# v's split parts stored by ScalarE in thirds, and k and q asked for later, in an attention and mixture-of-depths kernel

## The chip, the cores and the metric

The kernel runs on one core of a Trainium2 chip. Its metric is the device time of one execution in microseconds (us). Engines are named as the profile names them: PE (TensorE's matmuls), PEld (its weight loads), DVE (VectorE), ACT (ScalarE), POOL (GpSimd) and SP (SyncE, which here only issues transfers). Each takes its instructions in the order in which the program wrote them, and waits on semaphores where an operand is not ready. A transfer (DMA) is issued by SP, ACT or POOL and carried out by 16 DMA engines.

## The reference

An attention block whose keys and values are first condensed to 32 memory slots per head, and then a feed-forward block that works on 128 of the 576 rows of each batch. `q`, `k`, `v` are (8, 8, 576, 64), `phi` is (8, 8, 576, 32), all float32; the second block has width 512 and a hidden width of 1024.

```python
a = exp(phi - phi.max(axis=2)); a = a / (a.sum(axis=2) + 1e-9)     # softmax over the 576 rows
k_m, v_m = einsum('bhsm,bhsd->bhmd', a, k), einsum('bhsm,bhsd->bhmd', a, v)
scores = q @ k_m.transpose(0, 1, 3, 2) / 8
attn = softmax(scores)                                             # over the 32 slots
x = (attn @ v_m) with heads side by side                           # (8, 576, 512)
s = x @ w_gate
for b in range(8):
    top = the 128 rows of b with the largest s[b]
    out[b] = x[b]
    out[b, top] += sigmoid(s[b, top]) * (relu(x[b, top] @ w1) @ w2)
```

## The kernel before

The 64 pairs of batch and head are taken four heads at a time: 16 *groups* (b, g), numbered 0 to 15, two per batch.

**Softmax and keys** (`softmax`, L187, and `keys`, L306). A group's weights `a` are computed by DVE and ACT in turn on tiles of 128x576, with many correction steps. `load_phi` (L98) fetches phi when the group starts. `load_k` (L102, called at L228) fetches the group's k, 576 KB, into the tile `kb`. At the end `keys` transposes `a` on PE (L314), splits it on DVE in a coarse part and a rest (`big`, `low`, L320 and L322), has POOL store both parts to the DRAM tensor `aparts` (8 transfers, L325), and multiplies with `kb` on PE (L331) into `kbd`, the condensed keys.

**Splitting v** (`split_v`, L284). For each group a piece of v is loaded by SP into the tile `vb` (L291). DVE makes the coarse part `vhi` (L294) and the rest, in place in `vb` (L296). POOL stores both to the DRAM tensor `vparts` (L298), each written twice: a stored piece is twice what was read. The first nine groups go in whole pieces (1152 columns) with two buffers; the other seven go in halves (576 columns) with one buffer. Nothing reads `vb` afterwards but the two stores, so a buffer is free when both have landed.

**Sums of values** (`all_sums`, L355). v's condensed form needs more precision than one pass over the parts gives, so the parts of `a` and v are read back as rows spread over 32 partitions and multiplied by PE in a fixed order of rows (L382, tiles `acc`). There are four *stages*, each for two batches (four groups), and 32 pieces of 18 rows in a stage. `load_rows` (L341) has SP issue five transfers per piece: one of `v_rows` from vparts (L344) and four of `a_rows` from aparts (L351), into one of three sets of buffers. A stage's first rows are asked for when all its four groups have been done for five turns (L367), and its sums begin two turns after that at the earliest.

**Attention** (`attention`, L676). For a batch: `centre` (DVE, PE, ACT), `scores` (PE multiplies q with `kbd`, L490; ACT and DVE make exp minus one, L476 to L479), `attend` (PE L535 and L548, DVE L552, POOL or DVE L555, and POOL's stores of `out` and `xs`), `rank` (DVE and ACT find each row's rank) and `gather` (POOL fetches the chosen rows). q of the next batch is fetched by `load_q` (L106) into two buffers `qb`: at L683, in the two calls that follow the scores. A batch's attention may start when its sums are done, when fewer than two others are running, and 12 turns after the last start (8 when softmax is over).

**Feed-forward** (`ffn`, L636). PE's products with `w1_sb` (L654) and `w2_sb` (L664), and a scattered store into `out`.

**The order of the work** is written out by a loop of *turns* at the end of the kernel function. All the parts above are Python generators; each `yield` ends a *call*. A turn makes one call of softmax (two groups alternate in the first part, one runs alone later; a group takes ten calls), then perhaps one of `split_v`, then 7, 10 or 12 of `all_sums` (`steps`, L730; eight matmuls each), then one for each running attention, then two of the feed-forward. That order is the order of instructions on every engine and in every queue; times come out of it and of the waits. SP's queue therefore holds, turn by turn, the loads of phi and k, of v, of rows and of q. Counted by the yields, the loop has 226 turns. The first part ends at turn 83, when the odd groups below 8 are done: the tiles of the first part are given up, v goes on in halves, and attention may begin. Softmax is done in turn 160.

`split_v` has two yields per piece: a call that loads, and a call that splits and stores. It is called at every fourth turn in the first part and at every second later (L763). So a split comes four turns after its load, then two, and a group takes eight turns in both.

Of the kernel before, what the change touches and what calls it, by code (L numbers as in the profile page):

```python
# [39 lines left out]
def kernel(  # L40
# [15 lines left out]
    nc = tc.nc  # L56
# [45 lines left out]
    def load_k(i, ch):  # L102
        ks[i] = exs[ch].tile([PT, NC, D // NG], F32, name="kb")
        nc.sync.dma_start(out=ks[i], in_=k[groups[i]])

    def load_q(b, j):  # L106
        qs[b, j] = step.tile([P, NPR, S // 2], F32, name="qb")
        nc.sync.dma_start(out=qs[b, j], in_=qT[b, :, :, j * (S // 2):(j + 1) * (S // 2)])
# [78 lines left out]
    def softmax(i, ch):  # L187

        ex = exs[ch]

        def t(name, dtype=F32):

            return ex.tile([P, NC * P if name in WIDE else S], dtype, name=name)[:, :S]

        r = phis.pop(i)
        less_mx = ex.tile([P, 1], F32, name="mx")
        nc.vector.tensor_scalar(out=t("den"), in0=r, scalar1=-1.0, scalar2=None, op0=ALU.mult,
                                op1=ALU.min, accum_out=less_mx)
        nc.scalar.activation(r, r, AF.Identity, bias=less_mx)
        q = t("q", I16)  # L200
        act(q, r, LOG2E)
        yield
        for ln2 in (LN2_HI, LN2_LO):
            stt(out=r, in0=q, scalar=-ln2, in1=r, op0=ALU.mult, op1=ALU.add)

        rh, rl = t("rh", I16), t("rl")
        act(rh, r, 2.0 ** 11)
        num, den = t("num"), t("den")
        act(num, r, SQ[0], SQ[1], AF.Square)
        act(den, r, EXP_Q[2] * UP, EXP_Q[1] * UP)  # L210
        ends = t("lo"), t("big")
        act(ends[0], rh, -0.2734375 * UP * GRID, UP)
        act(ends[1], rh, UP * GRID / 4, EXP_P[1] * UP)
        yield
        stt(out=num, in0=num, scalar=SQ[2], in1=r, op0=ALU.add, op1=ALU.mult)
        act(num, num, 1.0, EXP_P[2] * UP)
        stt(out=rl, in0=rh, scalar=-GRID, in1=r, op0=ALU.mult, op1=ALU.add)

        def near(val, f, end):


            low = t("low")
            stt(out=low, in0=val, scalar=-f * UP, in1=r, op0=ALU.add, op1=ALU.mult)
            stt(out=low, in0=rl, scalar=f * UP, in1=low, op0=ALU.mult, op1=ALU.add)
            tt(out=val, in0=end, in1=low, op=ALU.add)

        yield
        load_k(i, ch)  # L228
        near(den, -0.2734375, ends[0])
        dh = t("dh", I16)  # L230
        act(dh, den, FINE)
        near(num, 0.25, ends[1])
        vh = t("vh", I16)
        act(vh, num, GRID)
        y0 = t("y0", I16)
        act(y0, r, 1.0, 14 * LN2, AF.Exp)
        inv = t("rl2")
        act(inv, r, INV[0], INV[1], AF.Exp)
        act(inv, inv, 1.0, INV[2] - 9 * LN2, AF.Exp)
        yield  # L240


        lo, big, low = t("lo"), t("big"), t("low")
        tt(out=low, in0=num, in1=rl, op=ALU.mult)
        stt(out=lo, in0=num, scalar=GRID, in1=vh, op0=ALU.mult, op1=ALU.subtract)
        tt(out=lo, in0=lo, in1=rh, op=ALU.mult)
        tt(out=big, in0=vh, in1=rh, op=ALU.mult)
        tt(out=low, in0=low, in1=lo, op=ALU.add)
        stt(out=num, in0=big, scalar=UP, in1=low, op0=ALU.add, op1=ALU.add)
        yield  # L250

        dl, p = t("lo"), t("big")
        stt(out=dl, in0=den, scalar=FINE, in1=dh, op0=ALU.mult, op1=ALU.subtract)
        tt(out=p, in0=y0, in1=dh, op=ALU.mult)
        tt(out=num, in0=num, in1=p, op=ALU.subtract)
        tt(out=dl, in0=y0, in1=dl, op=ALU.mult)
        tt(out=num, in0=num, in1=dl, op=ALU.subtract)
        two_q = t("den", I32)
        yield
        act(two_q, q, UP, 127 * UP, AF.Relu)  # L260
        tt(out=num, in0=num, in1=inv, op=ALU.mult)
        tt(out=num, in0=num, in1=y0, op=ALU.add)
        sm = ex.tile([P, 4], F32, name="sm")
        e = num
        stt(out=e, in0=num, scalar=FINE, in1=two_q.bitcast(F32),
            op0=ALU.mult, op1=ALU.mult, accum_out=sm[:, 0:1])

        nc.vector.tensor_scalar_add(sm[:, 0:1], sm[:, 0:1], 1e-9)
        nc.vector.reciprocal(sm[:, 1:2], sm[:, 0:1])  # L269
        nc.vector.tensor_single_scalar(sm[:, 2:3].bitcast(I32), sm[:, 0:1].bitcast(I32), -4096,  # L270
                                       op=ALU.bitwise_and)
        nc.vector.tensor_sub(sm[:, 3:4], sm[:, 2:3], sm[:, 0:1])
        nc.vector.tensor_scalar_mul(sm[:, 2:3], sm[:, 2:3], -1.0)
        a0 = t("vh", F16)
        nc.scalar.activation(a0, e, AF.Copy, scale=sm[:, 1:2])  # L275
        yield
        for part in (2, 3):
            stt(out=e, in0=a0, scalar=sm[:, part:part + 1], in1=e, op0=ALU.mult, op1=ALU.add)
        stt(out=e, in0=e, scalar=sm[:, 1:2], in1=a0, op0=ALU.mult, op1=ALU.add)  # L279
        soft[i] = e  # L280
        yield
        yield from keys(i, ch)

    def split_v(some, pool, cuts):  # L284

        n = 4 * S * Dh // P
        for b, g in some:
            for x0 in range(0, n, n // cuts):
                x = slice(x0, x0 + n // cuts)
                vb = pool.tile([P, n // cuts], F32, name="vb")  # L290
                nc.sync.dma_start(out=vb, in_=v[b, g, :, x])  # L291
                yield
                hi = pool.tile([P, n // cuts], F32, name="vhi")
                nc.vector.tensor_single_scalar(hi.bitcast(I32), vb.bitcast(I32), -4096,  # L294
                                               op=ALU.bitwise_and)
                nc.vector.tensor_sub(vb, vb, hi)  # L296
                for vp, src in enumerate((vb, hi)):
                    nc.gpsimd.dma_start(  # L298
                        out=vparts[b, g, :, vp].rearrange("w r s d -> w (r s d)")
                                               .rearrange("w (p x) -> p w x", p=P)[:, :, x],  # L300
                        in_=src.unsqueeze(1).to_broadcast([P, 2, n // cuts]))
                yield
# [52 lines left out]
    def all_sums():  # L355
# [7 lines left out]
        def load_some(end):  # L363
            while len(loaded) < min(end, len(pieces)):
                st, ch = pieces[len(loaded)]

                if not all(turn >= made.get(i, turn) + 5  # L367
                           for i in range(st * SET * NG, (st + 1) * SET * NG)):
                    break
                load_rows(len(loaded), st, ch)  # L370
                loaded.append(turn)
# [155 lines left out]
    def attend(b, general):  # L527
        eT, tg = eTs[b % 2], tgs[b % 3]
        row, rest = mean[b]
        for c0 in range(0, NT, 2):  # L530
# [5 lines left out]
                                     rhs=heads_of, start=True, stop=True)  # L536
            if working:
                yield
            rd = step.tile([P, 2, H], F32, name="rd")[:, :cols]
            nc.vector.tensor_scalar(out=rd.rearrange("p c (g h) -> p c g h", g=2), in0=den,  # L540
                                    scalar1=float(M), scalar2=1e-9, op0=ALU.add, op1=ALU.add)
# [134 lines left out]
    def attention(b, general=False):  # L676
        yield from centre(b)
        yield
        yield from (scores_less_max if general else scores)(b)
        for j in range(2):  # L680
            yield
            if not general and b + 1 < B:
                load_q(b + 1, j)  # L683
        yield from attend(b, general)
        yield
        yield from rank(b)
        for t in range(nt):
            yield from gather(b, t)
            chosen.append((b, t))
# [63 lines left out]
    while True:  # L753
# [6 lines left out]
        if working and next(working[0], working) is working:  # L760
            finish(working[1])
            working.clear()
        if working and turn % (2 if attend_all else 4) == 1:  # L763
            next(working[1], None)
        for _ in range(steps()):
            next(sums, None)
        if attend_all is None and set(order[1]) <= set(made):

            finish(working[1])
            first.close()  # L770
            work, step, one = (
                ctx.enter_context(tc.tile_pool(name=name, bufs=2 - (name == "one"),
                                               reuse_waits="tile"))
                for name in ("step", "work", "one"))
            vio = ctx.enter_context(tc.tile_pool(name="vio2", bufs=1, reuse_waits="tile"))
            working[1] = split_v(groups[two + 1:], vio, 2)
            for j in range(2):
                load_q(0, j)
            eTs = [one.tile([P, 2, NT * P], F32, name=f"eT{i}") for i in range(2)]
            for t in eTs:  # L780
                nc.gpsimd.memset(t[:, :, S:], 0.0)
            attend_all = attentions()
# [54 lines left out]
```

## Time and profile before

| | us |
|---|---|
| median of 9 runs (lowest to highest) | 914.66 (901.18 to 927.58) |
| the profiled execution | 910.61 |
| its span, first to last instruction | 908.8 |
| PE busy in it | 600.8 |
| DVE busy | 611.8 |
| ACT busy | 295.0 |
| POOL busy | 235.2 |
| the four stages of sums on PE, begin to end | 142 to 292, 296 to 435, 486 to 621, 667 to 782 |
| start of softmax of groups 8, 10, 12, 14 (DVE, L197) | 246, 333, 444, 547 |
| last group's weights done (DVE, L279) | 640 |

The profile is of one execution. A line of waits names the engine and line that waited, what ended the wait, and then the total, the number and the longest wait in us. SPq is SP's queue of transfers: a wait there holds back every transfer behind it. A line of a timeline gives the start and the length in us, the engine, the line, the operation and the tiles; an issue's length is the time of the issue, not of the transfer. The granted clock is the share of PE's full clock that it was allowed, and the DMA share is the mean busy share of the 16 DMA engines.

### The profile page before, as it was taken

Reading aid. Unit: us, or ns where it says so; the run is one execution under the profiler, and the core shown is the slowest. Engines: PE = TensorE matmul, PEld = TensorE weight load, DVE = VectorE, ACT = ScalarE, POOL = GpSimd, SP = SyncE. Lnnn points to the kernel's source line nnn. Section 1 sums busy time; section 2 is a strip of 40 time slices with the busy share of each in tenths; the row PEclk is TensorE's granted clock in tenths of the full one; section 3 lists DMA queues with packets and bytes.
Section 4 is the critical chain, followed back from the end, with each engine's and each line's share of the span. In section 5 each row is a group of like instructions: output and inputs, shape, how many; then the busy total and the mean of one; then the engine's idle time right before and its main releaser. Section 6 shows DMA issues by size and latency. Waiting matters only on the chain. (4 is left out here: it accounts for less than half of the span.)

```text
span 908.8 us, 25253 instructions
## 1 busy us (share of the span) xinstructions
PE 600.8 (66%) x10738; PEld 437.8 (48%) x10738; DVE 611.8 (67%) x1117; ACT 295.0 (32%) x578; POOL 235.2 (26%) x349
## 2 busy tenths in 40 slices
PE   0122333457764666795847879777889988888894
PEld 0122222456654546674614656565555675534541
DVE  4899888947973765759789695979844433527820
ACT  3434434324341513332433624343320210332230
POOL 7033321330220431251423324232501110112200
PEclk9999999656575766865667979975898978979598
DMA  5368936876767785878554778663356666223300
GB/s 167 143 195 286 302 119 207 267 241 190 236 178 222 235 252 180 265 228 264 186 190 139 223 219 251 202 186 123 84 153 192 180 200 202 57 76 114 118 25 15
DMA packets 61944, 166.10 MB, mean 183 GB/s; under 512 B 11136, under 2 KB 21376, under 8 KB 61824
## 3 DMA queue, kind: packets, MB, share of 16 engines
q1 hardware_dynamic: 40096, 94.14, 34.4%
q0 software_dynamic: 21728, 70.27, 23.6%
q8 instruction: 87, 1.43, 0.7%
q14 instruction: 33, 0.27, 0.1%
HBM read 96.21 MB, written 68.16 MB: 181 GB/s over the span
## 5 line engine op out<-in xcount | busy, mean ns | idle before, releaser
L382 PE MATMUL acc<-a_rows,v_rows 32*64 32x128 f32 x9216 | 220.6, 258 | 120.7 <-DMA a_rows<-aparts 94.5
L382 PEld LDWEIGHTS acc<-a_rows,v_rows 32*64 32x64 f32 x9216 | 199.3, 167 | 165.3 <-issue 104.2
L314 PE MATMUL bank<-ident,num 128*96 128x128 f32 x96 | 20.9, 380 | 105.1 <-DVE num L279 100.1
L331 PE MATMUL bank<-lo,kb 96*128 96x64 f32 x384 | 65.7, 349 | 20.9 <-ACT lo L316 19.4
L654 PE MATMUL bank<-w_sb,xeT 128*128 128x512 f32 x128 | 73.9, 714 | 4.8 <-ACT xeT L645 3.1
L331 PEld LDWEIGHTS bank<-lo,kb 96*128 96x128 f32 x384 | 63.6, 261 | 27.2 <-ACT lo L316 21.7
L325 POOL DMA_DIRECT2D aparts<-low x64 | 46.9, 740 | 103.9 <-DVE low L322 88.0
L298 POOL DMA_DIRECT2D vparts<-vb x23 | 16.9, 735 | 219.9 <-DVE vb L296 219.9
L314 PEld LDWEIGHTS bank<-ident,num 128*96 128x96 f32 x96 | 15.2, 176 | 109.4 <-issue 89.0
L548 PE MATMUL bank<-vbd,eT 128*128 128x256 f32 x160 | 61.7, 523 | 0.0
L664 PE MATMUL bank<-w_sb,hT 128*128 128x512 f32 x128 | 60.8, 609 | 0.0
L552 DVE TENSOR_TENSOR xj<-bank,rd 128x512 f32<-128x512 f32 x40 | 27.5, 688 | 42.2 <-PE bank L548 40.9
L601 DVE SCALAR_TENSOR_TENSOR cmp<-row,tg,wide 128x576 bf16<-128x576 f32 x40 | 32.5, 814 | 22.4 <-ACT row L587 21.6
L325 POOL DMA_DIRECT2D aparts<-big x64 | 46.5, 732 | 4.0 <-DMA vparts<-vhi 4.0
L548 PEld LDWEIGHTS bank<-vbd,eT 128*128 128x128 f32 x160 | 36.1, 250 | 17.4 <-issue 13.1
L654 PEld LDWEIGHTS bank<-w_sb,xeT 128*128 128x128 f32 x128 | 26.4, 223 | 32.3 <-issue 23.6
L555 POOL TENSOR_TENSOR xj<-xj,mean 128x1024 f32<-128x1024 f32 (+1 forms) x11 | 24.1, 2189 | 53.8 <-DVE xj L552 32.7
L275 ACT ACTIVATE vh<-num,sm 128x576 f16<-128x576 f32 x16 | 12.4, 776 | 76.8 <-DVE sm L269 55.1
L479 DVE SCALAR_TENSOR_TENSOR eT<-es,th 128x288 f32<-128x288 f32 x32 | 14.4, 450 | 32.7 <-ACT th L477 32.7
L336 ACT ACTIVATE kbd<-bank 64x64 f32<-64x64 f32 x32 | 7.0, 218 | 89.0 <-PE bank L331 88.8
L664 PEld LDWEIGHTS bank<-w_sb,hT 128*128 128x128 f32 x128 | 22.5, 189 | 25.9 <-issue 24.4
L560 POOL DMA_DIRECT2D out<-xj x24 | 16.3, 678 | 68.8 <-DVE xj L555 65.8
(149 smaller groups left out, 1157.8 us busy)
## 6 DMA issues: line engine op xcount, KB each, us to landing
v_rows<-vparts SPq DMA_DIRECT2D x128, 288.0 KB
a_rows<-aparts SPq DMA_DIRECT2D x512, 36.0 KB
vparts<-vb POOLq DMA_DIRECT2D x9, 1152.0 KB, 6.4
vparts<-vhi POOLq DMA_DIRECT2D x9, 1152.0 KB, 8.8
kb<-in_k SPq DMA_DIRECT2D x16, 576.0 KB
qb<-in_qT SPq DMA_DIRECT2D x16, 576.0 KB
out<-xj POOLq DMA_DIRECT2D x16, 512.0 KB, 4.0
xs<-xj POOLq DMA_DIRECT2D x16, 512.0 KB, 4.0
```

The source lines that it names most:

```text
L298: nc.gpsimd.dma_start(out=vparts[b, g, :, vp].rearrange("w r s d -> w (r s d)") .rearrange("w (p x) -> p w x", p=P)[:, :, x], in_=src.unsq ...
L314: nc.tensor.transpose(out=tp[:, c], in_=a[:, (c0 + c) * PT:(c0 + c + 1) * PT], identity=ident)
L325: nc.gpsimd.dma_start(out=aparts[h, b, g, part].rearrange("(c p) m -> p c m", p=PT), in_=src[:, :, h * M:(h + 1) * M])
L331: nc.tensor.matmul(out=km[:, rr], lhsT=kb[:, c, rr * P:(rr + 1) * P], rhs=aS[:, c, rr * 2 * M:(rr + 1) * 2 * M], start=(c == 0), stop=(c = ...
L382: nc.tensor.matmul(out=accs[i][:Dh, :P].rearrange("p (h m) -> p h m", m=M), lhsT=vr[p, s], rhs=ar[p, :, s], start=(ch == 0 and s == 0), st ...
L548: nc.tensor.matmul(out=o[:, g * 4 * Dh:(g + 1) * 4 * Dh], lhsT=eT[:, g, (c0 + c) * P:(c0 + c + 1) * P], rhs=vbd[b % 3][:, g], start=False, ...
L552: nc.vector.tensor_mul(x[:, c].rearrange("p (h d) -> p h d", d=Dh), o.rearrange("p (h d) -> p h d", d=Dh), rd[:, c].unsqueeze(2).to_broadc ...
L555: (nc.gpsimd if working else nc.vector).tensor_add(x, x, row.unsqueeze(1).to_broadcast([P, cols, D]))
L560: nc.gpsimd.dma_start(out=out[b, c0 * P:c0 * P + (cols - 1) * P + n].rearrange("(c p) d -> p c d", p=n), in_=x[:n])
L601: nc.vector.scalar_tensor_tensor(out=cmp, in0=row, scalar=g, in1=wide[:, off:off + S], op0=ALU.is_equal, op1=ALU.mult, accum_out=equal[:, ...
L654: nc.tensor.matmul(out=ps[:n], lhsT=xeT[:, d, :n], rhs=w1_sb[:, d, f0:f0 + 512], start=(d == 0), stop=(d == KD - 1))
L664: nc.tensor.matmul(out=ps[:n], lhsT=hT[:, f, :n], rhs=w2_sb[:, f], start=(f == 0), stop=(f == KF - 1))
```

## The change

The change has five parts. The stores of v's two parts are issued by ACT (`nc.scalar.dma_start`) instead of POOL, and a `yield` is put between the split and the stores, so that a piece takes three calls: load, split, store. `split_v` is called at every third turn in the first part and at every turn later; a group then takes nine turns in both. In the later part v goes in thirds (384 columns) instead of halves, with two buffers instead of one. `load_k` moves from softmax's fourth call to its sixth. `load_q` for the next batch, both halves, moves from the two calls after the scores into `attend`, behind the first matmuls of L535. And a stage's rows are asked for four turns after its groups are done instead of five. The layout of `vparts` and `aparts`, and the size of a piece of rows, stay.

```diff
@@ -225,7 +225,6 @@
             tt(out=val, in0=end, in1=low, op=ALU.add)
 
         yield
-        load_k(i, ch)
         near(den, -0.2734375, ends[0])
         dh = t("dh", I16)
         act(dh, den, FINE)
@@ -248,6 +247,7 @@
         tt(out=low, in0=low, in1=lo, op=ALU.add)
         stt(out=num, in0=big, scalar=UP, in1=low, op0=ALU.add, op1=ALU.add)
         yield
+        load_k(i, ch)
 
         dl, p = t("lo"), t("big")
         stt(out=dl, in0=den, scalar=FINE, in1=dh, op0=ALU.mult, op1=ALU.subtract)
@@ -294,8 +294,9 @@
                 nc.vector.tensor_single_scalar(hi.bitcast(I32), vb.bitcast(I32), -4096,
                                                op=ALU.bitwise_and)
                 nc.vector.tensor_sub(vb, vb, hi)
+                yield
                 for vp, src in enumerate((vb, hi)):
-                    nc.gpsimd.dma_start(
+                    nc.scalar.dma_start(
                         out=vparts[b, g, :, vp].rearrange("w r s d -> w (r s d)")
                                                .rearrange("w (p x) -> p w x", p=P)[:, :, x],
                         in_=src.unsqueeze(1).to_broadcast([P, 2, n // cuts]))
@@ -364,7 +365,7 @@
             while len(loaded) < min(end, len(pieces)):
                 st, ch = pieces[len(loaded)]
 
-                if not all(turn >= made.get(i, turn) + 5
+                if not all(turn >= made.get(i, turn) + 4
                            for i in range(st * SET * NG, (st + 1) * SET * NG)):
                     break
                 load_rows(len(loaded), st, ch)
@@ -536,6 +537,9 @@
                                      rhs=heads_of, start=True, stop=True)
             if working:
                 yield
+            if c0 == 0 and not general and b + 1 < B:
+                for j in range(2):
+                    load_q(b + 1, j)
             rd = step.tile([P, 2, H], F32, name="rd")[:, :cols]
             nc.vector.tensor_scalar(out=rd.rearrange("p c (g h) -> p c g h", g=2), in0=den,
                                     scalar1=float(M), scalar2=1e-9, op0=ALU.add, op1=ALU.add)
@@ -679,8 +683,6 @@
         yield from (scores_less_max if general else scores)(b)
         for j in range(2):
             yield
-            if not general and b + 1 < B:
-                load_q(b + 1, j)
         yield from attend(b, general)
         yield
         yield from rank(b)
@@ -760,7 +762,7 @@
         if working and next(working[0], working) is working:
             finish(working[1])
             working.clear()
-        if working and turn % (2 if attend_all else 4) == 1:
+        if working and (attend_all or turn % 3 == 1):
             next(working[1], None)
         for _ in range(steps()):
             next(sums, None)
@@ -772,8 +774,8 @@
                 ctx.enter_context(tc.tile_pool(name=name, bufs=2 - (name == "one"),
                                                reuse_waits="tile"))
                 for name in ("step", "work", "one"))
-            vio = ctx.enter_context(tc.tile_pool(name="vio2", bufs=1, reuse_waits="tile"))
-            working[1] = split_v(groups[two + 1:], vio, 2)
+            vio = ctx.enter_context(tc.tile_pool(name="vio2", bufs=2, reuse_waits="tile"))
+            working[1] = split_v(groups[two + 1:], vio, 3)
             for j in range(2):
                 load_q(0, j)
             eTs = [one.tile([P, 2, NT * P], F32, name=f"eT{i}") for i in range(2)]
```

## The prediction

> **What bounds the kernel now.** I read the page first, then the span cut at the borders of the four stages of sums, then the waits of the engines and of SP's queue, and last the timelines around single v and q loads. The cut (columns: PE, PEld, DVE, ACT and POOL busy us, granted clock, DMA share, GB/s):
>
> ```profile
> 142.00:284.00 142.00, 81.26 (x2304) 74.67 (x2308) 107.56 (x175) 48.76 (x78) 30.73 (x44) 0.65 0.73 223
> 284.00:436.00 152.00, 108.15 (x2638) 90.12 (x2631) 102.86 (x190) 47.18 (x95) 42.55 (x58) 0.66 0.76 238
> 436.00:486.00 50.00, 27.52 (x94) 17.05 (x93) 39.61 (x78) 18.07 (x38) 19.91 (x24) 0.64 0.48 157
> 486.00:640.00 154.00, 127.92 (x2635) 91.05 (x2635) 123.37 (x227) 60.13 (x123) 48.20 (x58) 0.82 0.64 197
> ...
> 667.00:782.00 115.00, 103.52 (x2498) 74.13 (x2502) 43.26 (x88) 15.69 (x36) 14.66 (x23) 0.88 0.62 185
> ```
>
> From 142 to 640 us no engine is full: DVE is busy 68 to 80%, PE 55 to 83%, and they wait for each other, because both take their work in the order written. While sums run the DMA engines are at 0.64 to 0.76. From 667 on PE is the bound (90%). Next, the waits that the change touches; first SP's queue, then the engines (total us, times, longest):
>
> ```profile
> SPq L291 <- DMA vparts<-vb: 106.5, 7, 28.6
> ...
> SPq L351 <- DMA aparts<-big: 66.0, 4, 38.8
> SPq L108 <- PE bank L490: 31.7, 2, 27.3
> SPq L104 <- PE bank L331: 20.8, 4, 13.7
> ```
>
> ```profile
> POOL vparts L298 <- DVE vb L296: 219.9, 18, 23.4
> ...
> PE acc L382 <- DMA a_rows<-aparts: 94.5, 46, 8.1
> ...
> DVE vhi L294 <- DMA vb<-in_v: 13.0, 5, 5.5
> ```
>
> The two largest, 106.5 and 219.9 us, look like the prize and are not. SP's waits for v's buffer begin at 5, 50, 60, 84, 429 and 444 us, the seventh is short (70.8 us of them before 102, when no row load exists; 35 us between 429 and 466, when the second stage's sums are over and the third begins only at 486). POOL's next instructions after a v store hang on DVE work that itself comes after the split. Neither sets the end. What does reach it: PE's 94.5 us for a_rows (with 10.1 for v_rows), and DVE's waits.
>
> **The change, part by part.** The profiled execution took 910.61 us (span 908.8 and 1.8 around it), 4.05 below the median of 914.66; I sum on 910.6 and add 4.05 at the end.
>
> *Stores from POOL to ACT.* POOL loses 46 issues of 0.72 us (33 us) and its 219.9 us of waiting. Worth nothing: POOL is busy 26%, and the items behind a store (aparts L325, the adds L555, los L443) wait for later DVE work. ACT gains 2x9 + 2x21 = 60 issues. The trace has no DMA issued by ACT; the nearest are SP's: 0.37 us (v load, L291), 0.50 (v_rows), 0.60 (q load). At 0.55 that is 33 us of ACT. ACT is busy 49 of 142 to 60 of 154 us while sums run, so a pair of 1.1 us meets something urgent about a third of the time: 30 pairs x 1.1 x 0.35 = 12 us, and of ACT's delays I let a third through, since DVE mostly waits for other things: **+4**, ends 0 (ACT idle) and +33 (all on the path). The store also waits for DVE's split in ACT's queue; the exps L476 and softmax's activations queue behind it. The added yield puts the store one call later (three turns before turn 84, one after), and in most calls ACT has by then waited for newer DVE work, so I add nothing for it beyond those ends.
>
> *Thirds.* The split's two instructions take 0.75 and 1.36 us at 1152 columns, 0.46 and 0.76 at 576; continued to 384 that is 0.36 and 0.56. 21 x 0.92 = 19.4 against 14 x 1.22 = 17.1 us of DVE: **+1**, ends 0 and +2.3. Stores: 1152 KB land in 6.4 us (vb), 576 KB in 4.8, so 384 KB in about 4.3 by the same line; a group's three pairs then occupy the queue longer than its two did, off the path while the buffer's next load comes four turns later.
> Here the Trainium skill speaks against the change: "DMA: Bandwidth & Descriptors", section "Anatomy of one DMA", gives about 2 us fixed per DMA plus size over 436 GB/s, so that cutting finer pays the fixed part more often. The two landings above agree in kind, with a larger fixed part (3.2 us). By the page's figures 14 more stores would cost an estimated 28 us of latency, all hidden if buffers suffice, so the sum is the same by either.
>
> *The v load's lead.* This I think decides. Counting yields: in the middle (turn 84 on) a call is made at every second turn now, load in one and split in the next, so the split follows its load by two turns. After the change a call is made each turn, so the split follows **one** turn after the load; the second buffer doesn't help, as the load isn't asked for earlier. (Before turn 84 the lead falls from four turns to three, and loads were mostly far ahead: left to the ends.) Two loads on SP and their splits on DVE:
>
> ```profile
> 292.62 0.37 SPq L291 DMA_DIRECT2D vb<-in_v  x1
> ...
> 309.38 0.37 SPq L291 DMA_DIRECT2D vb<-in_v  x1
> ```
>
> ```profile
> 297.41 0.61 DVE L294 TENSOR_SCALAR vhi<-vb 128x576 int32<-128x576 int32 x1
> ...
> 318.08 0.45 DVE L294 TENSOR_SCALAR vhi<-vb 128x576 int32<-128x576 int32 x1
> ```
>
> 4.8 and 8.7 us apart. Over the 14 pieces the distances are 6.4, 4.8, 8.7, 4.1, 5.6, 10.4, 6.2, 12.1, 11.1, 17.8, 22.6, 4.8, 12.2, 8.0; of these four ended in DVE's waits for vb (5.5, 4.0, 2.1, 0.6). A load that was waited for took 4.8 to 6.4 us; for two thirds of the bytes I estimate 4.5. A turn is 4.8 us (29 turns of the second stage's sums, 296 to 435). Less the old wait and one turn, distances fall to -4.0, 0, 3.9, -0.7, -3.2, 5.6, -0.6, 7.3, 6.3 and so on; short of 4.5 by 8.5, 4.5, 0.6, 5.2, 7.7, 0, 5.1, then 0 until the twelfth (5.1) and fourteenth (1.3): 38 us over 14 pieces, 57 over 21, against 12 now. That is a ceiling: once DVE is late it stays late, and the next load comes early for it; and in those stages DVE has 30% idle. A fifth of the added 45 reaches the end: **+8**, ends 0 and +25.
>
> *q later.* q for b+1 is asked for in turns 104/105 for use at 107 now (b=0), and then in 105, both, for use at 106; the same for b=2. The old second load on SP and the use on PE:
>
> ```profile
> 370.63 0.59 SPq L108 DMA_DIRECT2D qb<-in_qT  x1
> ```
>
> ```profile
> 376.41 0.71 PE L490 MATMUL bank<-qb,kbd 128*64 128x288 f32 x4
> ```
>
> The new place is behind that turn's row loads too (371.3 to 374.8), less what the moved issues free: about 373.5. With 5.9 us to land (the chain's "DMA qb<-in_qT" at 735) that is 379.4, 3 us late; for b=2 likewise 1.3. PE's acc, transposes and ffn queue behind the wait. Other b have 6 turns or more, or (b=6) wait for buffers as before. **+3**, ends 0 and +9. The 31.7 us of SP waiting for q's buffers (27.3 of it before 806 us, no rows left) stays and costs nothing.
>
> *k later.* From the 4th to the 6th of softmax's ten calls, used in the tenth. The last one: issued 616.6, used 644.2, 27.6 us for six turns; four turns leave 18 against 5.4 (a v load of the same 576 KB): **0**, end +3. SP's 20.8 us for kb's buffer shrinks; no row load was late for it.
>
> *Rows one turn earlier (5 to 4).* All of sums and attention move a turn ahead of softmax; the loop has 225 turns instead of 226. PE already stood 7.5 us waiting for the first rows at 142, so nothing there; at 486 an acc slot falls into a PE wait of 12.9 us. At the end one turn is 2.55 us:
>
> ```profile
> 659.88 1.98 PE L664 MATMUL bank<-w_sb,hT 128*128 128x512 f32 x4
> ...
> 662.42 1.98 PE L664 MATMUL bank<-w_sb,hT 128*128 128x512 f32 x4
> ```
>
> **-2.5**, ends -5 and 0.
>
> *Transfers.* v's traffic is spread over 9 turns a group for 8, bursts are two thirds as large, aparts no longer stand behind v in POOL's queue. Slow row issues on SP (1.5 us and more) follow v stores, as at 302 (store 301.3) and 357.6 (356.7). But bytes are equal and the third stage gets more of v. **-2**, ends -13 and +5.
> The same page, section "Issuing engines are not separate DMA queues", says issuing from several engines saves only the issuer's time; taken strictly this term would be 0 and the sum 2 higher. No DMA from ACT is in this trace to test it.
>
> Sum: 4+1+8+3+0-2.5-2 = +11.5; 922.1 on the profiled execution, **926** on the median (+1.2%).
>
> **Rivals.** *Rows arrive sooner (faster).* PE waits 104.6 us for rows. If smaller bursts take a quarter (26 us), half of it reaches the end (-13), and v and q loads cost nothing: -13+4+1-2.5 = -10.5, **904**. It decides from a fall of the a_rows wait to about 70 with vb's wait no higher than 13. For it: slow issues after stores. Against: DMA shares near 0.75 with the same bytes.
> *All cancels.* DVE's stalls fall where it would have waited for PE: 910.6-2.5+4+1+3-2 = 914, **918**.
> *ACT on the path.* The 42 issues of the middle, 23 us, all show instead of 4: **945**. For it: DVE waits for ACT in softmax's ping-pong. Against: most ACT idle time ends on DVE or PE.
> *The change doesn't do what it says* would be v's buffer wait staying on SP: four turns lie between store and next load, so I leave it no chance of its own.
>
> **Chances.** Forecast, slower by 1 to 2.7%: 0.40; ACT, beyond that: 0.10; cancelling, within 1% (about what a measurement of this kernel can tell from no change): 0.28; rows, faster: 0.22. Eight in ten reach from half-way below the rows case, 898, to just past ACT's, 950.
>
> **What would show it.** DVE L294's wait for vb rising from 13.0 to 25 or more, most in 284 to 436; a PE wait for qb at two places; SP's L291 wait gone with no gain; ACT with 60 issues near 0.55 us; a_rows waits within 15 of 94.5; third stage's sums starting one turn sooner. I am wrong if vb's wait stays small because DVE runs late anyway, or if ACT's issues are far longer than SP's.

## The result: 5.2% slower, outside the range

The changed kernel takes **954.44 us** (median of 10 runs, 948.6 to 960.04) against 911.11 for the kernel before beside it (31 runs, 899.5 to 927.58): ratio **1.0521**, 95% interval 1.0483 to 1.0558. The forecast was 926 with a range of 898 to 950. Ratios here leave out executions disturbed by the chip's state, so they are not always the quotient of the medians shown.

The profiled execution took 952.08 us, span 950.3, granted clock 0.80 (before: 910.61, 908.8 and 0.799). The work is the same: PE busy 598.7 us (600.8 before), DVE 615.1 (611.8), ACT 296.9 (295.0), POOL 203.4 (235.2, less its issues). So the 41.5 us are waiting. Where they arise is read from the end of each group's weights (DVE, L279): group 7 is done at 257 us instead of 249, group 11 at 472 instead of 436, group 15 at 688 instead of 640. The lag is 8, 36 and 48 us; what follows the last group takes 262 us instead of 269. All is lost before 688 us, most of it while v is split and rows are read.

The span of the changed kernel, cut at the borders of its own stages of sums (columns: begin and end, length, PE, PEld, DVE, ACT and POOL busy us, granted clock, DMA share, GB/s):

```profile
146.00:307.00 161.00, 80.65 (x2421) 74.27 (x2414) 100.41 (x158) 46.16 (x75) 23.53 (x34) 0.65 0.68 207
307.00:469.00 162.00, 100.30 (x2507) 82.88 (x2505) 102.89 (x194) 47.24 (x93) 31.44 (x44) 0.69 0.68 205
469.00:510.00 41.00, 30.16 (x95) 18.55 (x94) 38.98 (x75) 18.26 (x39) 17.26 (x20) 0.63 0.64 199
510.00:688.00 178.00, 137.06 (x2644) 96.24 (x2643) 132.32 (x247) 61.41 (x124) 47.19 (x53) 0.81 0.60 181
714.00:824.00 110.00, 100.00 (x2521) 73.17 (x2521) 43.30 (x88) 15.70 (x36) 14.71 (x23) 0.92 0.63 194
```

The first two stretches are 19 and 10 us longer than their counterparts before, with busy times about as before or lower; the third is 9 us shorter, and the fourth, with the third stage's sums, 24 us longer. The clock is lower by 0.01 at most. The DMA share in the first two *fell*, from 0.73 and 0.76 to 0.68: the engines that carry the transfers are busy for less of the time than before, and yet the rows come later. The last stretch, where softmax and v are over, is no longer than it was (110 us, 115 before).

Who waits in the changed kernel, in SP's queue and then on the engines (total us, times, longest):

```profile
SPq L352 <- DMA aparts<-big: 70.1, 6, 42.7
SPq L291 <- DMA vparts<-vb: 51.1, 6, 14.8
SPq L345 <- PE acc L383: 50.0, 28, 10.8
SPq L104 <- PE bank L332: 41.6, 3, 16.6
SPq L352 <- DMA vparts<-vb: 32.7, 6, 8.4
SPq L108 <- PE bank L491: 30.1, 2, 25.7
SPq L345 <- DMA vparts<-vb: 25.5, 5, 10.8
...
SPq L352 <- DMA vparts<-vhi: 8.1, 9, 2.9
```

```profile
PE acc L383 <- DMA a_rows<-aparts: 178.8, 62, 14.4
...
DVE vhi L294 <- DMA vb<-in_v: 67.3, 14, 9.3
...
PE bank L491 <- DMA qb<-in_qT: 7.2, 1, 7.2
```

Three things moved. PE's wait for `a_rows` rose from 94.5 to 178.8 us. DVE's wait for a loaded piece of v rose from 13.0 to 67.3. And SP's row loads have a wait that hardly existed before (0.7 us in all): L352, which is before's L351, and L345 wait for *stores of v*, 69.5 us together. In SP's queue of the kernel before, these are all the row loads' waits for such stores:

```profile
SPq L351 <- DMA vparts<-vhi: 0.5, 1, 0.5
...
SPq L351 <- DMA vparts<-vb: 0.2, 1, 0.2
```

The line to stop at is L352: the `a_rows` loads read `aparts` and write row buffers. They read nothing of `vparts`, and yet they stand still until a store into it has landed.

**Why they wait.** The records name the semaphore that each transfer raises when it has landed. In this program SP's transfers go round eight of them (numbers 100 to 103 and 106 to 109) in the order of the program: first, second, to eighth, and first again. Before, POOL's stores used eight others (110 to 117). After, ACT's 60 stores are on *SP's* eight: SP's 721 transfers and ACT's 60 together go round them without a gap. A transfer that raises a semaphore waits in its queue until the one that used it last, eight places before it, has landed. So a row load that comes eight places behind a store of ACT waits until ACT has got to that store, in its own order, and until the store has landed; everything behind it in SP's queue waits too. Followed through this rotation, 23 of the 69.5 us pass before ACT has issued the store, and 44 between its issue and its landing. SP's own issues did not get longer: they add up to 442 us, against 454 in the run sched_kq4 below, which is the changed kernel with POOL's stores.

One case, in the timelines of SP's, ACT's and PE's instructions of the changed kernel (start, length, engine, line, operation; x4 is four in a row):

```profile
383.29 0.50 SPq L345 DMA_DIRECT2D v_rows<-vparts  x1
383.83 3.27 SPq L352 DMA_DIRECT2D a_rows<-aparts  x4
387.20 0.39 SPq L291 DMA_DIRECT2D vb<-in_v  x1
392.95 0.50 SPq L345 DMA_DIRECT2D v_rows<-vparts  x1
393.84 2.45 SPq L352 DMA_DIRECT2D a_rows<-aparts  x4
396.34 1.28 SPq L108 DMA_DIRECT2D qb<-in_qT  x2
```

```profile
387.75 0.37 ACTq L299 DMA_DIRECT2D vparts<-vb  x1
388.16 2.72 ACTq L299 DMA_DIRECT2D vparts<-vhi  x1
```

```profile
400.64 1.23 PE L491 MATMUL bank<-qb,kbd 128*64 128x288 f32 x4 [7.21 <-DMA qb<-in_qT]
```

Between 387.6 and 392.95 SP issues nothing; the wait is put down to ACT's store of 387.75. That store and the `v_rows` load of 392.95 raise the same semaphore, 100. In the program the store stands before the load of `v_rows` that SP issued at 383.29, so ACT came to it some 4.5 us after SP had passed its place, and it then took 5.2 us to land. Queued behind stand the next rows and then q, issued at 396.34, and PE waits 7.21 us for q until 400.64. The store's lateness and its landing have become SP's wait, and then PE's. (The later request for q has a part in the last step: kq_only, below, shows a wait of 4.1 us for q without any store on ACT.)

### The profile page after: what moved, and what is told of

It is laid out like the page before. It is cut to its first block, busy times and chain, and to the rows that moved or that the text cites. A ratio compares the mean times of both kernels' runs of the same rounds, so it can differ in the third digit from the quotient of the medians.

```text
span 950.3 us, 25279 instructions
## 1 busy us (share of the span) xinstructions
PE 598.7 (63%) x10738; PEld 436.1 (46%) x10738; DVE 615.1 (65%) x1130; ACT 296.9 (31%) x578; POOL 203.4 (21%) x304
## 5 line engine op out<-in xcount | busy, mean ns | idle before, releaser
L383 PE MATMUL acc<-a_rows,v_rows 32*64 32x128 f32 x9216 | 221.2, 257 | 188.3 <-DMA a_rows<-aparts 178.8
L326 POOL DMA_DIRECT2D aparts<-low x64 | 47.0, 742 | 335.1 <-DVE low L323 325.4
L332 PE MATMUL bank<-lo,kb 96*128 96x64 f32 x384 | 61.4, 333 | 15.2 <-ACT lo L317 15.0
L332 PEld LDWEIGHTS bank<-lo,kb 96*128 96x128 f32 x384 | 59.6, 246 | 19.1 <-ACT lo L317 17.4
L294 DVE TENSOR_SCALAR vhi<-vb 128x384 int32<-128x384 int32 (+1 forms) x30 | 14.4, 481 | 67.3 <-DMA vb<-in_v 67.3
L559 POOL TENSOR_TENSOR xj<-xj,mean 128x1024 f32<-128x1024 f32 (+1 forms) x12 | 26.8, 2232 | 106.1 <-DVE xj L556 86.7
L326 POOL DMA_DIRECT2D aparts<-big x64 | 46.5, 735 | 0.0
L321 DVE TENSOR_SCALAR big<-lo 96x768 int32<-96x768 int32 x16 | 8.8, 551 | 48.0 <-ACT lo L317 48.0
L317 ACT ACTIVATE lo<-bank 96x384 f32<-96x384 f32 x32 | 14.6, 483 | 69.3 <-PE bank L315 69.1
L603 ACT ACTIVATE sign<-row,tg 128x576 bf16<-128x576 f32 x40 | 30.9, 774 | 3.3 <-issue 1.6
```

The costliest lines, as they stand in the source:

```text
L317: nc.scalar.activation(aS[:, c0:c0 + 3], tp, AF.Copy)
L326: nc.gpsimd.dma_start(out=aparts[h, b, g, part].rearrange("(c p) m -> p c m", p=PT), in_=src[:, :, h * M:(h + 1) * M])
L332: nc.tensor.matmul(out=km[:, rr], lhsT=kb[:, c, rr * P:(rr + 1) * P], rhs=aS[:, c, rr * 2 * M:(rr + 1) * 2 * M], start=(c == 0), stop=(c = ...
L383: nc.tensor.matmul(out=accs[i][:Dh, :P].rearrange("p (h m) -> p h m", m=M), lhsT=vr[p, s], rhs=ar[p, :, s], start=(ch == 0 and s == 0), st ...
L559: (nc.gpsimd if working else nc.vector).tensor_add(x, x, row.unsqueeze(1).to_broadcast([P, cols, D]))
L603: nc.scalar.activation(sign, row, AF.Sign, bias=g, scale=-1.0, accum_out=less[:, c:c + 1])
```

## The experiments

Kernels are named by their labels. Where a diff says "k, q, rows", it is the change's last three parts: k and q asked for later, rows four turns after a stage's groups. "The order of v" is the added yield, the call rates, the thirds and the two buffers.

### The three parts apart

**act**: the kernel before, and only the issuing engine changed.

```diff
-                    nc.gpsimd.dma_start(
+                    nc.scalar.dma_start(
                         out=vparts[b, g, :, vp].rearrange("w r s d -> w (r s d)")
```

> The kernel before with one edit: v's stores issued by ACT, in the same call as the split, halves, one buffer, everything else as before. Theory 1 (the v load comes only one turn ahead of the split, and DVE stands waiting): this edit leaves the lead at two turns, so within 1% of before, vb's wait on DVE near 13 us, a_rows waits near 95. Theory 2 (ACT's stores share the eight completion semaphores of SP's loads, so that a row load must wait until a v store has landed): most of the 43 us, 20 us or more, come with this edit alone; SP's row loads show waits on vparts of 40 us or more, and PE's a_rows wait rises above 130 us.

Measured 934.35 us, ratio 1.0352 (1.0254 to 1.045): **+32 us** for one word. PE's wait for `a_rows` is 137.7 us, DVE's for v 16.6. Of the 37.5 us that its row loads wait for stores of v, 4 pass before ACT has issued the store and 34 until it has landed. In SP's queue, where L351 is the load of `a_rows`:

```profile
SPq L351 <- DMA vparts<-vb: 20.7, 7, 7.6
SPq L351 <- DMA vparts<-vhi: 13.0, 9, 3.3
```

**sched**: the kernel before with the new order of v, stores left on POOL.

```diff
                 nc.vector.tensor_sub(vb, vb, hi)
+                yield
...
-        if working and turn % (2 if attend_all else 4) == 1:
+        if working and (attend_all or turn % 3 == 1):
...
-            vio = ctx.enter_context(tc.tile_pool(name="vio2", bufs=1, reuse_waits="tile"))
-            working[1] = split_v(groups[two + 1:], vio, 2)
+            vio = ctx.enter_context(tc.tile_pool(name="vio2", bufs=2, reuse_waits="tile"))
+            working[1] = split_v(groups[two + 1:], vio, 3)
```

> The kernel before with the new order of v's pieces alone: a yield between split and stores, every third turn and then every turn, thirds, two buffers; stores stay on POOL, k, q and rows as before. Theory 1: most of the 43 us, 25 us or more; vb's wait on DVE rises from 13 to 50 us or more. Theory 2: within 1% of before or a little slower (up to 12 us); the vb wait may rise but is absorbed, and SP's row loads do not wait for vparts.

Measured 901.77 us, ratio 0.9989 (0.994 to 1.0039): nothing. The waits of its engines:

```profile
PE acc L383 <- DMA a_rows<-aparts: 105.0, 38, 12.3
...
DVE vhi L294 <- DMA vb<-in_v: 34.6, 10, 10.7
```

DVE does wait 22 us longer for v than before, as the prediction said it would; these 22 us cost nothing.

**kq4**: k, q, rows alone.

```diff
         yield
-        load_k(i, ch)
         near(den, -0.2734375, ends[0])
...
         yield
+        load_k(i, ch)
...
+            if c0 == 0 and not general and b + 1 < B:
+                for j in range(2):
+                    load_q(b + 1, j)
             rd = step.tile([P, 2, H], F32, name="rd")[:, :cols]
...
         for j in range(2):
             yield
-            if not general and b + 1 < B:
-                load_q(b + 1, j)
...
-                if not all(turn >= made.get(i, turn) + 5
+                if not all(turn >= made.get(i, turn) + 4
```

> The kernel before with k and q asked for later and rows asked for one turn earlier, nothing else. Both theories 1 and 2: within 1% of before, between 5 us faster and 5 us slower; a wait of PE for qb of up to 9 us in total at one or two places. A third theory (q's late load is the main loss) needs 20 us or more here.

Measured 900.38 us, ratio 0.9935 (0.9869 to 1.0002). So neither this part nor the order of v loses anything by itself; the loss comes with ACT's stores.

**act_sched**: the first two together, the changed kernel without k, q, rows.

> Stores on ACT and the new order of v's pieces together; k, q and rows as before. Theories 1 and 2 both expect nearly the whole loss, 36 to 48 us slower than before (947 to 959). If the two add up (theory 1 and 2 each a part) it is the sum of the two runs alone; if it is far above that sum, they work only together; if it is much below 36 us, k, q and the earlier rows carry a part.

Measured 969.55 us, ratio 1.0715 (1.0617 to 1.0813): **+65 us**, twice the sum of its parts (3.5% and 0). SP's loads of `a_rows`:

```profile
SPq L352 <- DMA vparts<-vb: 63.1, 12, 14.9
...
SPq L352 <- DMA vparts<-vhi: 14.8, 12, 2.3
```

The two parts are not independent. The order of v that costs nothing with POOL's stores costs as much again with ACT's. Of the row loads' 90.1 us, 31 now pass before ACT has issued the store (4 in act) and 57 until it has landed (34 in act). ACT does not stand longer behind the split itself: directly before its stores it waits 19 us for DVE, 35 in act. Which piece of the new order, the added yield, the call rates or the thirds, makes the stores late for SP is not shown.

**sched_kq4**: the changed kernel with the stores back on POOL, one word different.

```diff
-                    nc.scalar.dma_start(
+                    nc.gpsimd.dma_start(
```

> The changed kernel with the one word put back: v's stores on POOL. Theory 2: the whole loss goes, 892 to 915, within 1% of before or faster. If it stays above 925, the order of v's pieces and ACT's issue lose independently.

Measured 894.88 us, ratio 0.9858 (0.9778 to 0.9938): faster than the kernel before, 60 us faster than the changed one. In SP's queue this is the only wait of a row load for a store of v:

```profile
SPq L345 <- DMA vparts<-vhi: 2.3, 1, 2.3
```

### Is it ACT's waiting, the stores' bytes, or the shared semaphores?

**act_next**: ACT stores, with halves, one buffer and the old lead of the load, but the store one call after the split.

```diff
                 nc.sync.dma_start(out=vb, in_=v[b, g, :, x])
                 yield
+                yield
...
                 nc.vector.tensor_sub(vb, vb, hi)
+                yield
...
-        if working and turn % (2 if attend_all else 4) == 1:
+        if working and (attend_all or turn % 2 == 1):
```

> Stores on ACT as in the run act, but each pair is issued one call after its split (two turns in the first part, one in the middle), so that ACT no longer stands waiting for DVE's split; load-to-split lead, halves, one buffer and eight turns a group as before. Theory 2a (the v stores hold completion semaphores that SP's row loads need): the loss of act, 32 us, stays, 22 us or more; SP's row loads still wait 30 us or more for vparts. Theory 2b (ACT's queue stands behind DVE's split, 35 us in act): the loss falls to 12 us or less.

Measured 925.0 us, ratio 1.0162 (1.008 to 1.0243). The loss of act is about halved, which none of the theories had as its number; the row loads' wait, 40.6 us, is no shorter than act's. Its profiled execution lies 10 us above its median, so its waits (`a_rows` 147.1 us) say little.

**wait_only**: the kernel before, and after POOL's stores two one-column activations on ACT that read DVE's split. ACT waits for the split, and issues no transfer.

```diff
+                for vp, src in enumerate((vb, hi)):
+                    nc.scalar.activation(pool.tile([P, 1], F32, name=f"sc{vp}"), src[:, :1], AF.Copy)
```

> The kernel before, v's stores on POOL, and behind each split two activations of one column on ACT that read the split's results: ACT waits for DVE where it waited in the run tiny, but it issues no transfer. Theory L (SP's row loads take their turn on eight completion semaphores shared with ACT's transfers, and so wait until ACT has come to its transfer and the transfer has landed): within 8 us of before, no loss. Theory W (ACT standing behind DVE delays softmax by itself): 15 to 23 us slower, as tiny.

Measured 907.04 us, ratio 1.0012 (0.9969 to 1.0055). By the gaps in its queue ACT stands 36.6 us before these activations, about as long as it stood behind the split in act (35 us), and it costs nothing; the waits of its engines are those of the kernel before:

```profile
PE acc L384 <- DMA a_rows<-aparts: 95.5, 46, 7.9
...
DVE vhi L294 <- DMA vb<-in_v: 12.2, 4, 5.4
```

So ACT's waiting alone is not the loss.

**tiny**: the same place, but instead of the activations two transfers of one column each, issued by ACT. v itself still goes by POOL.

```diff
+                for vp, src in enumerate((vb, hi)):
+                    nc.scalar.dma_start(out=pool.tile([P, 1], F32, name=f"sc{vp}"), in_=src[:, :1])
```

> The kernel before, v's stores on POOL, with two additional transfers of one column (512 bytes) issued by ACT behind each split, from the same tiles and so with the same waits for DVE, into tiles that nothing reads. It puts the waits, the issues and two short uses of the shared semaphores on ACT, and nothing that lands late. Theory 2a: within 8 us of before. Theory 2b (waits and issues on ACT cost it): 20 us or more slower.

Measured 930.4 us, ratio 1.0246 (1.0163 to 1.0329). Transfers of 512 bytes, which nothing reads, bring most of act's loss; theory 2a, as it was put there, had within 8 us and is wrong, for the stores' bytes are not needed. SP's row loads (L346 `v_rows`, L353 `a_rows`) wait for them by name, and no row load reads `sc`:

```profile
SPq L353 <- DMA sc<-vb: 20.4, 7, 10.1
SPq L353 <- DMA sc<-vhi: 14.8, 6, 3.6
...
SPq L346 <- DMA sc<-vb: 4.3, 3, 2.6
```

**tiny_free**: tiny with a constant as its source (`ident`), so that ACT waits for no split.

> The run tiny with a constant as the source of its two transfers: ACT issues them in the same places, with no wait for DVE. Theory L: 6 to 20 us slower than before, because SP still waits for ACT to reach its place in its own order; SP's row loads wait 15 us or more for the small transfers. Theory W: within 6 us of before.

Measured 926.4 us, ratio 1.0242 (1.0146 to 1.0339). In SP's queue, and then the transfers themselves by their line (ns: shortest, median, longest issue; first and last start):

```profile
SPq L346 <- DMA sc<-ident: 15.1, 4, 10.2
SPq L353 <- DMA sc<-ident: 8.9, 5, 5.2
```

```profile
L303 ACTq DMA_DIRECT2D sc<-ident x46: 472/494/1250, 24.3 to 566.1; - x46
```

The waits for these transfers fall from 39.5 to 24.0 us, the time hardly; at 22 us the loss is a little above Theory L's 6 to 20. A transfer that ACT issues in its own order is enough to make SP wait: 10 of the 24 us pass before ACT has come to it, 14 until it has landed.

**tiny_sp**: the same 46 constants issued by SP, in SP's own order.

> The run tiny_free with its two small transfers issued by SP instead of ACT, in the same places of the order, from the same constant: as many issues and as many uses of the shared semaphores, but no second engine between them. Theory L (a row load waits until another engine has come to its transfer): within 6 us of before, SP's own 46 issues of about 0.4 us being mostly covered. If the number of transfers on the eight semaphores is what costs, 15 us or more slower, as tiny_free.

Measured 920.78 us, ratio 1.0138 (1.0099 to 1.0177). It was to be within 6 us of before and is 12 above: a miss. The waits of row loads for `sc` are gone. What takes their place is SP's own time:

```profile
L303 SPq DMA_DIRECT2D sc<-ident x46: 471/599/2273, 3.6 to 560.4; - x46
```

The lengths of the 46 issues add up to 36 us of SP, and the time is 12 us longer. The step from tiny_free to tiny_sp is therefore not a clean price of the semaphores; the waits named in the queue are what shows them.

### Does the load's lead decide?

**lead**: the changed kernel, with a piece's load asked for in the call that splits the piece before it, three turns ahead instead of one. The helper `load` makes the tile and issues the transfer, as the two removed lines did.

```diff
...
-                vb = pool.tile([P, n // cuts], F32, name="vb")
-                nc.sync.dma_start(out=vb, in_=v[b, g, :, x])
+                vb = asked.pop(0) if asked else load(b, g, x)
                 yield
...
                 nc.vector.tensor_sub(vb, vb, hi)
+                todo.pop(0)
+                if cuts > 1 and todo:
+                    asked.append(load(*todo[0]))
                 yield
```

> The changed kernel with v's next load asked for in the call of the split before it, three turns ahead of its own split instead of one, in the middle part; stores on ACT and the rest as changed. Theory 1 as a part (the short lead doubles the loss that ACT's stores make): vb's wait on DVE falls from 67 to 25 us or less and the time to 925 to 940. If DVE's wait only stands for row loads being late at the same time, the wait falls and the time stays at 945 to 960.

Measured 936.0 us, ratio 1.0326 (1.026 to 1.0393). DVE's wait for v falls below before's, and 18 us of the 43 come back:

```profile
PE acc L394 <- DMA a_rows<-aparts: 151.4, 59, 14.1
...
DVE vhi L302 <- DMA vb<-in_v: 11.3, 4, 6.9
```

SP's row loads still wait 51.1 us for v's stores.

**lead_pool**: the same with POOL's stores.

> The changed kernel with v's stores on POOL and v's next load asked for in the call of the split before it, as in the run lead. DVE's wait for vb, 29.5 us in the run sched_kq4, falls below 12. If that wait reaches the end there as it does with ACT's stores, 880 to 888; if it is covered, as with sched against before, 888 to 898.

Measured 894.16 us, ratio 0.9888 (0.9794 to 0.9983), against 0.9858 without the lead. With POOL's stores the lead is worth nothing, although DVE's wait falls from 29.5 to 8.5 us.

### The small parts

**four_only** and its repeat: only the rows' turn, 5 to 4. **kq_only**: only k and q later. **sched_four**: the order of v and the rows' turn.

> The kernel before with a stage's rows asked for four turns after its groups instead of five, nothing else. The prediction's step gives -2.5 us, ends -5 and 0. If the gain of the run kq4 (about 6 us) comes from this part it is 4 to 8 us faster; if from k and q, within 3 us of before.

> The kernel before with k and q asked for later, nothing else. four_only was 1.2% faster and the three parts together (kq4) 0.65%: the prediction's steps give 0 and +3 us, so within 6 us of before, rather slower.

> The changed kernel without ACT's stores and without the later k and q: new order of v's pieces on POOL, and rows asked for one turn earlier. If the parts add up as the runs alone gave them (sched 0, four_only -1.2%, k and q +0.7%), it is 1.0 to 2.2% faster than before, at or below the run sched_kq4.

| | us | ratio (interval) |
|---|---|---|
| four_only | 896.73 | 0.9883 (0.9802 to 0.9964) |
| four_only_again | 895.59 | 0.987 (0.982 to 0.9919) |
| kq_only | 916.16 | 1.007 (1.0024 to 1.0116) |
| sched_four | 909.67 | 0.9981 (0.9947 to 1.0015) |
| sched_kq4_again | 896.04 | 0.9853 (0.9799 to 0.9908) |

> The kernel before with rows asked for one turn earlier, once more. If the 1.2% is real it is 0.6 to 1.8% faster than before; the prediction's step gives -2.5 us, 0.3%.

> The changed kernel with v's stores on POOL, once more and beside four_only on one chip. If its 1.4% is real it is 0.8 to 2% faster than before again; if small differences of this kernel move with chip and run, as sched_four against four_only suggests, it is within 0.7% of before.

Rows one turn sooner gain 11 us by themselves, k and q later lose 6, and together (kq4) they give 0.9935, as the sum would. The gain of the rows is gone when the order of v joins it (sched_four), and is back with k and q as well (sched_kq4, twice). Two forecasts missed: four_only gained more than either of its two ranges, and sched_four, forecast 1.0 to 2.2% faster, is as fast as before. The parts do not add, and no run here says why. What stands is that the changed kernel with its stores left on POOL is 1.5% faster than the kernel before.

## Why the prediction was wrong, and where it was right

**The step that failed is "Stores from POOL to ACT"**, priced at +4 with ends 0 and +33. Alone it measured +32 us, at its upper end; with the new order of v the two measured +65; and with all the other parts in place the same word is 60 us (after against sched_kq4), beyond its end. The prediction counted 60 issues at 0.55 us, 33 us in all, and asked only what stands behind them in *ACT's* queue. The count was right. This is the answer on line L299 of the changed kernel (ns: shortest, median, longest issue; first and last start),

```profile
L299 ACTq DMA_DIRECT2D vparts<-vb x30: 366/367/420, 35.1 to 624.6; - x30
L299 ACTq DMA_DIRECT2D vparts<-vhi x30: 369/483/2722, 35.5 to 625.0; - x30
```

and the 60 lengths add up to 31 us, since some issues are far above the median. ACT's waiting for the split costs nothing (wait_only). The prediction did not ask who in *SP's* queue waits for a transfer of ACT. Before, nobody on SP waited for a store of v but v's own loads (but for 0.7 us); after, the row loads wait 69.5 us. The rival "ACT on the path" had the sign and, at 945, the nearest time, but by all of ACT's issues in the middle showing: these are 23 us, as it counted, and the loss is 41, or 60 against the same kernel with POOL's stores. That it came near is in part luck.

The runs in order of what their row loads wait for v's stores or the added transfers:

| run | row loads' wait, us | PE's wait for a_rows, us | ACT's issues, us in all | ratio |
|---|---|---|---|---|
| tiny_sp | 0 | 121.8 | none | 1.0138 |
| wait_only | 0.6 | 95.5 | none | 1.0012 |
| sched_kq4 | 2.3 | 118.6 | none | 0.9858 |
| tiny_free | 25.0 | 138.6 | 26.7 | 1.0242 |
| act | 37.5 | 137.7 | 25.2 | 1.0352 |
| tiny | 39.5 | 142.3 | 29.0 | 1.0246 |
| act_next | 40.6 | 147.1 | 24.0 | 1.0162 |
| lead | 51.1 | 151.4 | 31.3 | 1.0326 |
| after | 69.5 | 178.8 | 31.3 | 1.0521 |
| act_sched | 90.1 | 179.2 | 28.8 | 1.0715 |

The loss grows with the row loads' wait, not in strict order: act, tiny and lead change places within their intervals' width or little more, and act_next lies too low. PE's wait for `a_rows` is no price by itself: sched_kq4 has 118.6 us of it and is faster than the kernel before. That the row loads' wait exists, that it needs only a transfer issued by ACT and not its bytes, and that it goes when the stores go back to POOL, is shown. One rival is not excluded as a part: ACT's own issuing, which nothing here separates from the shared semaphores, because wait_only puts no transfers on ACT, and tiny_sp pays on SP what it saves on ACT. In tiny_free it is 26.7 us, about as much as the loss. It cannot be the whole, for it stays between 24 and 31 us while the loss runs from 15 to 65. A run with ACT's stores on semaphores of their own would tell; there is none. Why act_next loses only half, and why k, q, rows take act_sched's 1.0715 down to 1.0521 when they are worth 0.9935 alone, stays open too.

**The v load's lead** ("This I think decides", +8). The mechanism came: DVE's wait rose to 67.3 us, 38.0 of it between 307 and 469. The price did not: with POOL's stores it is 0 (sched, -1 with an interval of about 4.5 us either way), and giving the lead back gains nothing (lead_pool). "DVE has 30% idle" was the right reason to let little through, and even a fifth was too much. It matters only with ACT's stores, where giving it back takes the ratio from 1.0521 to 1.0326. The two terms depend on each other; a sum of terms had no place for that.

**Thirds** (+1): nothing that can be told apart, by sched (0.9989). The rule of the Trainium skill cited there ("DMA: Bandwidth & Descriptors", section "Anatomy of one DMA") was fitted on transfers issued by GpSimd, as the stores of before and sched are. The fastest landings of `vb`'s stores that the records tell are 4.8 us for 1152 KB and 3.4 for 576 in before, and 2.9 for 384 in sched; by the page's figures they would be an estimated 4.7, 3.4 and 2.9. The prediction's larger fixed part, 3.2 us, came from the medians, 6.4 and 4.8, taken while other transfers ran. If the finer cut pays its fixed part more often, that is hidden in sched.

**POOL's 219.9 us and SP's 106.5 us of waiting are no prize**: right. L291's wait fell to 51.1 us and POOL's waiting for the split became waiting for its next work (`aparts` at L326 now waits 325.4 us for DVE); no time is seen to come of either.

**q later** (+3, ends 0 and +9) and **k** (0): +6 by kq_only, inside. SP's wait for k's buffer shrank there as forecast, from 20.8 to 6.3 us; in the changed kernel it is 41.6, and with POOL's stores 53.8 in a kernel that is faster. In kq_only PE waits for q at two places, forecast with 3 and 1.3 us; the line is from the waits of kq_only's engines:

```profile
PE bank L490 <- DMA qb<-in_qT: 4.9, 2, 4.1
```

**Rows one turn earlier** (-2.5, ends -5 and 0): -11 us alone, outside its ends. The prediction priced only the turn taken off the end, 2.55 us; where the rest comes from no run here separates.

**Transfers** (-2): the DMA share fell by 0.05 to 0.08 in the first two stretches and the rows came later, so nothing points to bandwidth as what was short. The rival "rows arrive sooner" had `a_rows` falling to 70; it went to 178.8. The sign "a_rows waits within 15 of 94.5" was wrong for the same reason as the first step, and "third stage's sums starting one turn sooner" did not come: they start at 510 us instead of 486. The Trainium skill's rule cited there ("DMA: Bandwidth & Descriptors", section "Issuing engines are not separate DMA queues"), that a second issuing engine saves only issuing time, has to be read with act beside it: here moving the stores to ACT cost 32 us, and the row loads' waits come from an ordering that the rule does not speak of.

## What to carry to other kernels

When a transfer moves to another engine, look up which semaphore it raises and which queue draws on the same ones: a transfer's place in that rotation is a dependency, and the profile shows it as a wait for a tile that the waiting instruction never touches. Be wary where a queue whose order is time-critical (here SP's rows) shares its rotation with an engine that comes to its transfers late, or whose transfers land late. And price two edits together when one makes late what the other waits for: 0 and 3.5% became 7%.

## What the runs showed of the hardware that was not expected

SP and ACT's transfers, in this program as built, share eight completion semaphores in one rotation; POOL's have eight of their own. Even 46 transfers of ACT of 512 bytes each, with ready sources, cost 22 us (tiny_free), their issuing included. A transfer of 512 bytes holds up a row load as a store of v does, if by less: 24 us in all, 14 of them landing. SP, which is never counted as busy, has so little slack for row loads that 36 us of added issues made the time 12 us longer (tiny_sp). The median issue on ACT took 0.37 to 0.49 us (after, tiny_free), that of a constant on SP 0.60 (tiny_sp).
